# Another order of steps in the head and middle of a fused block: the last fold of Wk ahead of the first values

## The chip, the core and the metric

One core of a Trainium2 chip runs the whole program. Its engines work side by side, each through its own queue of instructions in order: TensorE (PE, with its weight loads as PEld), VectorE (DVE), ScalarE (ACT), GpSimd (POOL) and SyncE (SP), which issues nearly all DMA transfers. An instruction that waits holds everything behind it in its engine's queue. Matmul results go to PSUM, eight banks of 512 float32 numbers in each of 128 partitions; the other engines move them to SBUF. The metric is the device time of one execution in microseconds (us); lower is better. A measurement is a median over several executions.

## What is computed

A pre-norm transformer block with linear attention and a feed-forward part, on 2048 tokens of width 640 in bf16, with 32 heads of width 20:

```python
qkv = (layernorm(x) @ wqkv)                    # q, k, v: 32 heads of 20
pq, pk = q @ w_phi, k @ w_phi                  # a 20x20 matrix for each head
phi_q = concat(softmax(pq), softmax(-pq))      # 40 features
phi_k = concat(softmax(pk), softmax(-pk))
kv  = phi_k^T @ v                              # summed over all tokens
z   = sum over tokens of phi_k
o   = (phi_q @ kv) / (phi_q @ z + 1e-6)
h   = x + o @ wo
out = h + silu(layernorm(h) @ w1) @ w2         # inner width 1728
```

## The kernel before

**Tiles and stages.** Tokens come in 16 tiles of 128, the width in five chunks of 128. The stages overlap: a head (first 11 us or so) in which w_phi is multiplied into the key part of wqkv, so that keys come out as features at once; a middle (to about 68 us) that makes keys K and values V of each tile, exponentiates and scales the keys and adds them into kv (two PSUM banks, 6 and 7); then queries, attention, the out projection and the feed-forward part, which follow in the same list and run to the end.

**Order by hand.** Every piece of work is a named step, a small function that emits a few instructions. One string, ORDER (lines 18 to 61), lists all 897 names; line 1097 walks through it and calls each step. The scheduler is in manual mode, so each engine gets its instructions in exactly this order, and the semaphores that keep data right are put in by the framework. A name's place in the list therefore sets its place only in the queues of the engines that it uses. ON (line 159) says on which engine some steps run.

**Steps of the head.**
- `warm0` to `warm17` (line 231): matmuls of constants that only keep TensorE busy, two banks of kv as target.
- `X0`, `X1`, `X2`, `X4`, `X8` (line 178): loads of 1, 1, 2, 4 and 8 tiles of x. `WK0` to `WK4` and `WV0` to `WV4` (line 181): loads of the five chunks of Wk and Wv, 160 KB each. `wph0`, `wph1` (lines 379, 381), `wq0` to `wq5` (line 425): w_phi once more, and transposed loads of the query part. All are issued by SP; WPH, the first load of w_phi, by ACT (line 183).
- `phi_a`, `phi_b` (lines 305, 308): DVE spreads w_phi into blocks; phi_a begins with the difference WPD.
- `wkC` (line 321): five transposes of a chunk of Wk into PSUM; `wkeC` (line 338): its copy to WTk, on DVE or ACT; `fkC` (line 345): six matmuls of it with phi, the fold; `fkCe` (line 354): the copy to Wfk on ACT.
- `stT` (lines 478, 479): mean and variance of a tile on DVE, three instructions; `rsT`: the inverse deviation, on POOL with a power (lines 487, 490) or on ACT (484, 485); `xnT` (line 494): the normalised tile on DVE or POOL; `xtT`: its transpose, by TensorE for tiles 0 to 3 (line 530) with `xT` (line 550) as copy, by a DMA (line 552) for the others.
- `V0.C` (line 583): tile 0's values, chunk by chunk, two matmuls each that need chunk C of Wv; `K0.C` (line 598): the same for keys. `K0s` takes a pair of PSUM banks.

**Steps of the middle.** `KT`, `VT` (line 571): ten matmuls of a tile with Wfk or Wv; `exT` (line 626): two exponentials on ACT into one of five EK buffers; `suT` (line 630): their sums on DVE; `rkT` (lines 638, 639): inverses on ACT; `scT` (line 643): the scaling on DVE, in place; `veT` (line 647): values to SBUF on ACT; `kvT` (line 662): eleven matmuls of scaled keys and values; `refT` (line 247) and `onesT` (lines 250, 252, 247): constants in buffers, on POOL. `mask`, `mask0` and `own` are masks on POOL; `phq` (line 402 on) spreads w_phi for the queries on POOL; `fqR`, `fqRe` (lines 437, 443) fold it into the query weights; `load0` to `load10` (line 563) load wo, w1 and w2.

**PSUM.** Six of the eight banks go round in three pairs (line 124): each wk pair, fold, xt, K and V takes the next pair and waits until the copy or exponential that empties its former use is done. The order in which the steps stand in ORDER thus also decides which step waits for which copy.

Of the kernel before, what the change touches and what calls it, by code (L numbers as in the profile page):

```python
# [15 lines left out]


ORDER = """
warm0 warm1 warm2 warm3 warm4 warm5 warm6 warm7 warm8 warm9 warm10 warm11 warm12 warm13 warm14 warm15
warm16 X0 WK2 st0 wk2 ones5 WK3 phi_a warm17 WK0 wke2 X1 phi_b wk3 mask fk2 wke3 ones4 WK1 WK4 wk0 rs0  # L20
xn0 xt0 fk2e wk1 X2 WV0 WV3 st1 X4 wke0 wke1 WV2 fk3 wph0 wk4 ones0 rs1 ones3 fk3e WV1 pad0 ones1 x0
wke4 fk0 fk1 V0.0 fk0e fk4 xn1 xt1 V0.3 WV4 fk1e K0s K0.2 st2 st3 fk4e K0.1 wph1 x1 mask0 K0.0 st4 rs3
own K0.4 rs2 xn2 K0.3 ex0 K1 V0.2 rs4 xn3 st6 xt2 ex1 V0.1 wq3 V1 wq0 xt3 x2 rs6 V0.4 ve1 X8 st5 xn4 su0
xn6 su1 rk0 sc0 x3 xt4 st7 K2 ve0 V2 ex2 st9 rs5 wq1 xn5 st10 ve2 K3 xt5 kv0 ex3 rs7 V3 rk1 ve3 st8
ones2 sc1 phq xn7 su2 K4 ex4 st14 V4 fq0 V5 rs8 ve4 fq0e xt6 kv1 su3 rk2 ve5 rs9 fq3 ref6 fq3e sc2 wq2
ref5 K5 xt7 su4 K6 ex5 kv2 st11 V6 xn8 xn9 ex6 st12 rk3 ref7 fq2 sc3 wq4 su5 K7 ve6 rk4 xt8 xt9 fq2e ex7
sc4 V7 rs10 su6 xn10 kv3 rs11 rs12 fq1 V8 ve7 kv4 su7 fq1e zeros ref8 fq4 ve8 V9 rk5 K8 fq4e rk6 ref9
ve9 sc5 xn12 kv5 sc6 rk7 ex8 wq5 st13 K9 fq5 sc7 ones6 ex9 load7 xt10 kv6 rs14 ref10 xn11 rs13 fq5e su8
Q0 kv7 st15 su9 eqr0 rk8 K10 qe0 V10 xn13 sc8 Q1 xn14 rs15 ex10 qs0 xt12 V12 kv8 ve10 rk9 sc9 ref13 qe1
su10 load9 ql0 ve12 load3 qs1 rk10 sc10 xt11 ref12 kv9 ref11 xt13 K12 xn15 K11 ex12 su12 K13 load1 ex11  # L30
ex13 load10 V11 kv10 xt14 su11 K14 ql1 load4 qi0 ve11 eqr1 V13 rk11 eqp su13 qi1 rk12 sc11 kv11 qr1
ref14 xt15 rk13 qr0 sc12 K15 ex14 su14 load0 Q2 ve13 kv12 sc13 ref15 ex15 rk14 su15 qe2 V14 rk15 V15
ve14 load5 Q3 kv13 sc14 mask1 kv14 ve15 sc15 qt1 qs2 load2 kv15 bd0 Q7 qt0 ql2 load6 load8 qi2 Q5 qe3
halves bd1 D0 D1 qr2 qe7 qe5 Q4 qs3 ql3 E0 Q10 E1 qi3 qr3 qs5 qe4 qe10 qt2 Q6 ql5 D2 ot0 qs4 qe6 ot1 Q9
qi5 ql4 qi4 qr5 qt3 qt5 E2 G00 qe9 G01 ga0 lm0 qr4 G11 ot2 G10 ls0 Q11 lr0 D3 qs6 qe11 Q8 ga1 E3 lm1 qt4
hn0 qs7 ot3 D5 E5 ls1 Q13 G20 qe8 lr1 ht0 G21 hn1 qe13 Q14 ht1 ga2 Q15 qr6 qs8 qe14 Q12 G31 qe15 qr7 D4
G30 qr8 E4 ot5 qt6 qe12 u0.L padL0 T3.0 u0.4 ga3 u0.6 qs9 s0.L G50 G51 D6 T1.1 T1.2 ga5 lm2 s0.4 s0.6
ls2 qt7 lm5 T2.2 u0.0 u0.8 s0.0 T3.2 ot4 s0.8 D7 lr2 lm3 E6 u0.12 ls5 qt8 u0.2 s0.2 padL1 E7 T4.2 S3.0
G41 ls3 T1.0 ot6 T3.1 lr5 G40 u0.10 D8 ga4 p7.0 T2.1 E8 G61 hn2 ot7 T2.0 lt0 hn5 lr3 lm4 s0.12 T4.1 G60
T4.0 s0.10 p1.0 p2.0 G71 r7.0 S1.0 ht2 r1.0 S2.0 G70 qr9 ht5 p6.0 S4.0 ls4 hn3 p4.0 r2.0 lr4 p5.0 hn4  # L40
w11.0 p3.0 ga6 ht3 w21.0 ht4 u2.6 qs11 r3.0 u2.10 w22.0 qt9 u2.L u2.9 ot8 w12.0 s2.10 qr11 ga7 u2.7 qs10
lm6 s2.6 qr10 D9 ls6 qs12 G81 qt11 s2.7 s2.L u2.4 s2.9 u2.1 G80 E9 lm7 ga8 qr12 qt10 u2.5 s2.1 lm8 u2.3
lt2 qt12 qs13 u2.2 s2.5 s2.4 D10 s2.3 ls7 u2.0 s2.0 u2.12 E10 lr6 ot9 s2.12 ot10 D11 u2.8 qr13 s2.2
u2.11 qs14 E11 s2.8 s2.11 G90 S3.2 ls8 G91 D12 p7.2 qr14 G101 ga9 hn6 r7.2 S1.2 lm9 lr7 p1.2 qt13 ot11
D13 ls9 E12 S2.2 G100 lr9 lr8 hn7 p2.2 r1.2 qt14 p6.2 ga10 G110 w11.2 r2.2 p4.2 hn9 ht6 ot12 ht9 G111
ht7 E13 S3.4 D14 hn8 w21.2 S4.2 ga11 p5.2 w22.2 p7.4 lm11 ht8 r3.2 lm10 E14 ot13 ls10 S1.4 p1.4 r7.4
p3.2 r1.4 out0 S2.4 out1 G121 u6.L G120 p6.4 qs15 u6.8 ga12 G131 ot14 r2.4 p5.4 s6.8 qr15 lm12 ls11 G130
p4.4 w21.4 lr10 u6.12 ga13 out3 qt15 lr11 w22.4 out5 s6.12 u6.5 w12.2 G140 ls12 r3.4 D15 s6.L u6.4 lt6
hn10 lr12 ht10 hn11 G141 u6.0 ga14 E15 lm13 ls13 u6.11 s6.5 p2.4 s6.11 hn12 s6.4 u6.7 u6.10 u6.9 u6.2
s6.10 s6.2 u6.6 ot15 s6.0 s6.7 w11.4 lr13 G151 hn13 u6.3 s6.6 S4.4 ht11 ht12 s6.9 s6.3 G150 u6.1 ht13  # L50
p3.4 u10.L s6.1 S3.6 lm14 u10.7 ga15 u10.12 p7.6 s10.7 S3.8 S1.6 s10.L lt10 lm15 w12.4 ls14 u10.0 u10.2
p1.6 r1.6 u10.4 ls15 s10.2 out2 s10.12 u10.6 lr14 lr15 r7.6 hn15 hn14 S2.6 p6.6 S4.6 ht15 p2.6 s10.0
p4.6 r2.6 p3.6 p5.6 ht14 w21.6 u10.8 s10.4 r3.6 u10.3 u10.1 w22.6 w11.6 u14.L p7.8 s10.8 s10.3 w12.6
out4 s10.6 S1.8 r7.8 p1.8 u14.0 u10.10 u10.5 r1.8 s10.5 s14.L s10.1 out6 S2.8 p6.8 S4.8 u10.11 r2.8 p5.8
S3.10 u10.9 s10.9 p4.8 s10.11 w21.8 p2.8 u14.10 s14.0 w22.8 s10.10 r3.8 p3.8 p7.10 w11.8 u14.4 S1.10
u14.2 p2.10 p1.10 out7 S2.10 s14.2 w12.8 r7.10 s14.10 p4.10 u14.12 r1.10 p6.10 S4.10 u14.8 S3.12 s14.4
r2.10 w21.10 p5.10 S1.12 u14.6 p1.12 out9 w11.10 p3.10 S2.12 p2.12 r3.10 r1.12 s14.8 out8 w11.12 p6.12
# [1077 lines left out]
```

## Time and profile before

| | |
|---|---|
| median of 3 runs | 225.18 us (224.81 to 225.22) |
| the profiled execution's own time | 225.49 us |
| its span, first to last instruction | 223.8 us |
| granted TensorE clock, mean | 0.998 |
| TensorE busy | 218.2 us |
| DVE, ACT, POOL busy | 173.0, 144.4, 70.2 us |

The 1.7 us between the profiled time and its span lie before the first and behind the last instruction. Busy times are unions of an engine's instructions; ends of matmuls are modelled, so that a busy TensorE may still lose up to about 0.15 us between two matmuls unseen. In a timeline a row gives start and duration in us, engine, line, operation, what it writes and reads, the number of merged instructions, and in brackets the idle time before it and what ended that. In the rows of one line or tile three durations are minimum, median and maximum in ns.

### The profile page before, as it was taken

The numbers are of one execution on the slowest core, as the hardware profiler recorded it, in microseconds if no ns is written. First come the engines' busy times: TensorE is split into PE (matmuls) and PEld (weight loads), VectorE is DVE, ScalarE is ACT, GpSimd is POOL, SyncE is SP. The second block draws the span as 40 slices with busy tenths as digits, with TensorE's granted clock in tenths as the row PEclk, the third lists the DMA queues.
The fourth block names the chain that finished last, engine by engine and source line by source line (L and its number), as shares of the span: only waits on it lengthen the run. The fifth ranks groups of instructions, "written<-read, shape, count | busy, mean of one in ns | idle before, by whom it ended". The sixth has DMA issues, their size and how long they took to land.

```text
span 223.8 us, 5031 instructions
## 1 busy us (share of the span) xinstructions
PE 218.2 (98%) x1926; PEld 154.8 (69%) x1935; DVE 173.0 (77%) x305; ACT 144.4 (65%) x321; POOL 70.2 (31%) x136
## 2 busy tenths in 40 slices
PE   8799999999999999999999999999999999999994
PEld 5677777777777777887655577665455656778773
DVE  4899999999989999999999999944024344436694
ACT  2799999999979899997086774268568332321000
POOL 6789899899000130163020130132004000000000
PEclk9999999999999999999999999999999999999999
DMA  6994639679999874935536666434512410010012
GB/s 174 320 263 134 114 77 165 185 190 161 315 201 175 175 134 81 213 56 107 126 78 139 126 145 124 120 95 81 63 29 53 91 60 0 29 44 0 29 62 88
DMA packets 68158, 26.98 MB, mean 121 GB/s; under 512 B 61159, under 2 KB 67111, under 8 KB 68007
## 3 DMA queue, kind: packets, MB, share of 16 engines
q1 hardware_dynamic: 67335, 26.61, 53.3%
q8 instruction: 15, 0.25, 0.5%
q10 hardware_dynamic: 800, 0.06, 0.3%
q14 instruction: 8, 0.07, 0.1%
HBM read 9.55 MB, written 2.62 MB: 54 GB/s over the span
## 4 chain that ended last, share of the span: by engine, by line
PE 94%; DMA 2%; SPq 2%; issue 0%; DVE 0%
PE banks L931 25%; PE banks L1036 24%; PE banks L571 18%; PE banks L849 10%; PE banks L609 9%; PE banks L817 3%; PE banks L662 2%; DMA Wv<-in_A_wqkv_dram 2%; PE banks L942 1%; SPq L181 1%; PE banks L583 1%; PE banks L437 1%; PE banks L598 1%; SPq L178 1%; PE banks L530 0%
## 5 line engine op out<-in xcount | busy, mean ns | idle before, releaser
L931 PE MATMUL banks<-HnT,w_sb 128*128 128x512 bf16 (+1 forms) x316 | 60.0, 335 | 0.4
L954 ACT ACTIVATE shT<-banks 128x512 bf16<-128x512 f32 (+1 forms) x53 | 29.1, 586 | 45.8 <-PE banks L931 44.8
L931 PEld LDWEIGHTS <-w_sb 128*128 128x128 bf16 x325 | 31.2, 98 | 21.2
L571 PEld LDWEIGHTS <-XnT 128*128 128x128 bf16 x300 | 28.5, 98 | 9.5
L494 POOL TENSOR_SCALAR xn<-X,mv,rs 128x640 bf16<-128x640 bf16 x12 | 30.6, 2550 | 1.7 <-ACT rs L485 1.4
L1036 PEld LDWEIGHTS <-S 128*128 128x128 bf16 x224 | 21.6, 98 | 8.8
L1044 DVE TENSOR_TENSOR r<-banks,X 128x320 f32<-128x320 f32 x32 | 15.4, 487 | 15.7 <-PE banks L1036 13.2
L516 POOL TENSOR_SCALAR rs<-mv 128x1 f32<-128x1 f32 x16 | 3.9, 244 | 73.8 <-ACT xn L509 73.5
L1036 PE MATMUL banks<-T,S 128*128 128x320 bf16 x168 | 26.1, 299 | 0.0
L849 PE MATMUL banks<-wo_sb,OT 128*128 128x320 bf16 x160 | 25.5, 299 | 0.1
L737 DVE TENSOR_REDUCE Sq<-EQ 128x66 f32<-128x1320 bf16 x16 | 24.2, 1519 | 0.0
L609 PE MATMUL banks<-Wfq,XnT 128*128 128x342 bf16 (+2 forms) x160 | 22.7, 293 | 0.0
L571 PE MATMUL banks<-Wv,XnT 128*128 128x320 bf16 x150 | 22.7, 299 | 0.0
L1051 DVE TENSOR_TENSOR o_t<-banks,r 128x320 bf16<-128x320 f32 (+2 forms) x33 | 14.9, 473 | 9.9 <-PE banks L1036 9.6
L630 DVE TENSOR_REDUCE Sk<-EK 128x64 f32<-128x1216 bf16 x16 | 22.2, 1403 | 0.1
L733 ACT ACTIVATE EQ<-banks 128x342 bf16<-128x342 f32 (+2 forms) x52 | 21.5, 526 | 0.4 <-PE banks L609 0.3
L1036 PEld LDWEIGHTS <-shT 128*128 128x128 bf16 x175 | 16.8, 98 | 6.6
L571 PE MATMUL banks<-Wfk,XnT 128*128 128x304 bf16 x150 | 21.3, 292 | 0.0
L626 ACT ACTIVATE EK<-banks 128x608 bf16<-128x608 f32 x32 | 20.3, 697 | 1.0 <-PE banks L571 0.5
L849 PEld LDWEIGHTS <-OT 128*128 128x128 bf16 x160 | 15.3, 98 | 6.7
L1018 DVE TENSOR_TENSOR S<-shT 128x896 bf16<-128x896 bf16 x16 | 9.8, 619 | 12.5 <-ACT shT L954 8.8
L609 PEld LDWEIGHTS <-XnT 128*128 128x128 bf16 x160 | 15.0, 97 | 5.4
(97 smaller groups left out, 329.2 us busy)
## 6 DMA issues: line engine op xcount, KB each, us to landing
out_dram<-o_t SPq DMA_DIRECT2D x15, 160.0 KB, 1.8
w_sb<-in_B_w_dram SPq DMA_DIRECT2D x5, 432.0 KB, 5.7
w_sb<-in_B_w_dram SPq DMA_DIRECT2D x3, 480.0 KB, 6.6
X<-in_A_x_dram SPq DMA_DIRECT2D x1, 1280.0 KB, 5.9
Wk<-in_A_wqkv_dram SPq DMA_DIRECT2D x5, 160.0 KB, 3.5
Wv<-in_A_wqkv_dram SPq DMA_DIRECT2D x5, 160.0 KB, 5.8
wo_sb<-in_A_wo_dram SPq DMA_DIRECT2D x1, 800.0 KB, 5.1
X<-in_A_x_dram SPq DMA_DIRECT2D x1, 640.0 KB, 6.5
```

What stands on the lines that cost most here:

```text
L494: eng.tensor_scalar(out=xn_[t][:], in0=X[:, t, :], scalar1=mv_.pop(t)[:, 0:1], scalar2=rs_.pop(t)[:], op0=ALU.subtract, op1=ALU.mult,)
L571: nc.tensor.matmul(ps[:, g, 0:w], XnT[:, c, t * P : (t + 1) * P], W[:, c, g * w : (g + 1) * w], start=(c == 0), stop=(c == C - 1),)
L609: nc.tensor.matmul(ps[:, 0 : e - a], XnT[:, c, t * P : (t + 1) * P], Wfq[:, c, a:e], start=(c == 0), stop=(c == C - 1),)
L626: nc.scalar.activation(E5[:, :, :, b, 0:DR], p4, AF.Exp, scale=sign)
L630: nc.vector.tensor_reduce(sk[t][:], ek[t][:, 0 : H * HF].rearrange("p (q f) -> p q f", f=DH)[:, :, 0:DR], axis=AX.X, op=ALU.add)
L733: nc.scalar.activation(features(t, a, b)[:, :, :, i, 0:DR], p4, AF.Exp, scale=sign)
L737: nc.vector.tensor_reduce(sq[t][:], EQ[0][:, t, :, 0:FCH].rearrange("p c (q f) -> p c q f", f=DH), axis=AX.X, op=ALU.add)
L849: nc.tensor.matmul(ps_of["G", t][:, g, 0:HD], ot[t][:, c, :], wo_sb[:, c, g * HD : (g + 1) * HD], start=(c == 0), stop=(c == C - 1),)
L931: nc.tensor.matmul(ps[:, at : at + n], w1_sb[:, c, fc * P : fc * P + P], HnT[u][:, c, 0:n], start=(c == 0), stop=(c == C - 1),)
L954: nc.scalar.activation(rows_of(u)[:, f0 * n : f1 * n], ps_of.pop(("u", u, f0))[:, 0 : (f1 - f0) * n], AF.Silu)
L1036: nc.tensor.matmul(ps[:, lo:hi], left[:, c, :], right[:, c, lo:hi], start=(c == 0 and k in FIRST), stop=(c == KS - 1 and k in LAST), skip_ ...
L1044: nc.vector.tensor_tensor(r_[t, name][:], ps_of[bank, t][:, 0:HD], X[:, t + i, g * HD : (g + 1) * HD], op=ALU.add)
```

## The change

Only ORDER changes, and only its first third: the same 897 names, from the first up to `rk12 kv11 qr1 ref14 xt15` in other places, the rest (from `rk13` on) word for word as it was. No instruction is added or taken away. On TensorE the order changes from

```
... wk2 warm17 wk3 fk2 wk0 xt0 wk1 fk3 wk4 fk0 fk1 V0.0 fk4 xt1 V0.3 K0.2 K0.1 K0.0 K0.4 K0.3 K1
V0.2 xt2 V0.1 V1 xt3 V0.4 K2 V2 K3 kv0 V3 K4 V4 fq0 V5 kv1 fq3 K5 K6 kv2 ...
```

to

```
... warm17 wk2 wk3 fk2 wk0 xt0 wk1 fk3 wk4 fk0 fk1 fk4 xt1 V0.0 V0.3 K0.2 K0.1 K0.0 K0.4 K0.3 K1
V0.2 xt2 V1 V0.1 xt3 V0.4 V2 K2 K3 V3 kv0 kv1 V4 K4 fq0 V5 fq3 kv2 K5 K6 ...
```

On DVE phi_a comes ahead of st0, and xn2 ahead of st4. On SP the order of the first twelve loads (up to `X4 WV2`) stays; behind them it was `wph0 WV1 WV4 wph1 wq3 wq0 X8 xt4 wq1 xt5 ...` and becomes `WV1 WV4 wph1 wq0 X8 wph0 wq3 wq5 xt4 xt5 ...`; `load1`, `load10` and `load4` come earlier among the transposes xt10 to xt15, `load3` later. On POOL the memsets of `mask`, `ones0` and the mask's first side come ahead of rs0, those of `ones4`, `ones3` and `pad0` later.

```diff
-warm0 warm1 warm2 warm3 warm4 warm5 warm6 warm7 warm8 warm9 warm10 warm11 warm12 warm13 warm14 warm15
-warm16 X0 WK2 st0 wk2 ones5 WK3 phi_a warm17 WK0 wke2 X1 phi_b wk3 mask fk2 wke3 ones4 WK1 WK4 wk0 rs0
-xn0 xt0 fk2e wk1 X2 WV0 WV3 st1 X4 wke0 wke1 WV2 fk3 wph0 wk4 ones0 rs1 ones3 fk3e WV1 pad0 ones1 x0
-wke4 fk0 fk1 V0.0 fk0e fk4 xn1 xt1 V0.3 WV4 fk1e K0s K0.2 st2 st3 fk4e K0.1 wph1 x1 mask0 K0.0 st4 rs3
-own K0.4 rs2 xn2 K0.3 ex0 K1 V0.2 rs4 xn3 st6 xt2 ex1 V0.1 wq3 V1 wq0 xt3 x2 rs6 V0.4 ve1 X8 st5 xn4 su0
-xn6 su1 rk0 sc0 x3 xt4 st7 K2 ve0 V2 ex2 st9 rs5 wq1 xn5 st10 ve2 K3 xt5 kv0 ex3 rs7 V3 rk1 ve3 st8
-ones2 sc1 phq xn7 su2 K4 ex4 st14 V4 fq0 V5 rs8 ve4 fq0e xt6 kv1 su3 rk2 ve5 rs9 fq3 ref6 fq3e sc2 wq2
...
+warm0 warm1 mask warm2 warm3 warm4 warm5 warm6 phi_a warm7 warm8 warm9 warm10 warm11 warm12 ones5 warm13
+warm14 warm15 warm16 ones0 X0 WK2 WK3 warm17 wk2 st0 wk3 wke2 mask0 phi_b rs0 WK0 X1 WK1 wke3 xn0 fk2
+ones1 wk0 WK4 own xt0 st1 wk1 fk2e fk3 wke1 ones3 wke0 X2 WV0 x0 ones4 wk4 wke4 fk0 rs1 fk3e xn1 fk0e
+WV3 fk1 fk4 fk1e xt1 X4 K0s pad0 V0.0 fk4e st2 st3 rs2 V0.3 K0.2 WV2 x1 K0.1 K0.0 K0.4 rs3 K0.3 xn3 xn2
+ex0 WV1 st4 WV4 K1 rs4 xn4 V0.2 st5 wph1 ex1 wq0 xt2 V1 st6 V0.1 X8 x2 xt3 ve1 rs5 xn5 V0.4 x3 su0 V2
+rk0 K2 ve2 rs6 wph0 su1 wq3 st7 xn6 rk1 ve0 K3 ex2 wq5 ex3 xt4 V3 ve3 sc1 sc0 rs7 kv0 kv1 ones2 st8 xt5
+phq ref5 rs8 su2 xt6 wq2 wq1 xn7 rk2 st9 xt7 V4 sc2 ve4 su3 K4 fq0 xn8 V5 ex4 fq3 fq0e ref6 wq4 kv2 ve5
...
```

More of the change, by code (lines that the diff above doesn't have):

```diff
@@ L24 @@
-xn6 su1 rk0 sc0 x3 xt4 st7 K2 ve0 V2 ex2 st9 rs5 wq1 xn5 st10 ve2 K3 xt5 kv0 ex3 rs7 V3 rk1 ve3 st8
-ones2 sc1 phq xn7 su2 K4 ex4 st14 V4 fq0 V5 rs8 ve4 fq0e xt6 kv1 su3 rk2 ve5 rs9 fq3 ref6 fq3e sc2 wq2
-ref5 K5 xt7 su4 K6 ex5 kv2 st11 V6 xn8 xn9 ex6 st12 rk3 ref7 fq2 sc3 wq4 su5 K7 ve6 rk4 xt8 xt9 fq2e ex7
-sc4 V7 rs10 su6 xn10 kv3 rs11 rs12 fq1 V8 ve7 kv4 su7 fq1e zeros ref8 fq4 ve8 V9 rk5 K8 fq4e rk6 ref9
-ve9 sc5 xn12 kv5 sc6 rk7 ex8 wq5 st13 K9 fq5 sc7 ones6 ex9 load7 xt10 kv6 rs14 ref10 xn11 rs13 fq5e su8
@@ L29 @@
[L29 to L53, printed above, removed]
@@ L54 @@
-out4 s10.6 S1.8 r7.8 p1.8 u14.0 u10.10 u10.5 r1.8 s10.5 s14.L s10.1 out6 S2.8 p6.8 S4.8 u10.11 r2.8 p5.8
+warm0 warm1 mask warm2 warm3 warm4 warm5 warm6 phi_a warm7 warm8 warm9 warm10 warm11 warm12 ones5 warm13
+warm14 warm15 warm16 ones0 X0 WK2 WK3 warm17 wk2 st0 wk3 wke2 mask0 phi_b rs0 WK0 X1 WK1 wke3 xn0 fk2
+ones1 wk0 WK4 own xt0 st1 wk1 fk2e fk3 wke1 ones3 wke0 X2 WV0 x0 ones4 wk4 wke4 fk0 rs1 fk3e xn1 fk0e
+WV3 fk1 fk4 fk1e xt1 X4 K0s pad0 V0.0 fk4e st2 st3 rs2 V0.3 K0.2 WV2 x1 K0.1 K0.0 K0.4 rs3 K0.3 xn3 xn2
@@ new lines @@
+ex0 WV1 st4 WV4 K1 rs4 xn4 V0.2 st5 wph1 ex1 wq0 xt2 V1 st6 V0.1 X8 x2 xt3 ve1 rs5 xn5 V0.4 x3 su0 V2
+rk0 K2 ve2 rs6 wph0 su1 wq3 st7 xn6 rk1 ve0 K3 ex2 wq5 ex3 xt4 V3 ve3 sc1 sc0 rs7 kv0 kv1 ones2 st8 xt5
+phq ref5 rs8 su2 xt6 wq2 wq1 xn7 rk2 st9 xt7 V4 sc2 ve4 su3 K4 fq0 xn8 V5 ex4 fq3 fq0e ref6 wq4 kv2 ve5
+st12 su4 fq3e K5 rk3 rs9 K6 ex5 st11 sc3 V6 xt8 ex6 fq2 rk4 ve6 kv3 st10 K7 V7 xn9 ref7 su5 rs10 ref8
+fq2e xn10 xt9 fq1 ex7 ve7 fq1e load7 V8 zeros fq4 rs12 rk5 ve8 st13 load1 fq4e sc4 kv4 V9 su6 rk6 ve9
@@ new lines @@
+xn12 ref9 fq5 rs11 su7 K8 sc5 sc6 xt10 kv5 st14 K9 fq5e ones6 st15 eqr0 rs13 load9 ex8 kv6 Q0 xn11 rs14
+load10 su8 ex9 rk7 xt12 V10 qe0 ref10 rk8 xn13 xt11 K10 su9 rs15 sc7 V12 sc8 load4 rk9 ve10 qs0 Q1 ex10
+ve12 xt13 sc9 xn14 ref11 su10 kv7 xt14 ref12 qe1 ql0 qs1 K12 kv8 K11 ex12 kv9 K13 ref13 V11 rk10 ql1
+ex11 xn15 ex13 su12 sc10 qi0 kv10 ve11 load3 su11 ref14 K14 V13 rk11 su13 qi1 eqr1 sc11 kv11 eqp rk12
+xt15 qr1 rk13 qr0 sc12 K15 ex14 su14 load0 Q2 ve13 kv12 sc13 ref15 ex15 rk14 su15 qe2 V14 rk15 V15 ve14
@@ new lines @@
+load5 Q3 kv13 sc14 mask1 kv14 ve15 sc15 qt1 qs2 load2 kv15 bd0 Q7 qt0 ql2 load6 load8 qi2 Q5 qe3 halves
+bd1 D0 D1 qr2 qe7 qe5 Q4 qs3 ql3 E0 Q10 E1 qi3 qr3 qs5 qe4 qe10 qt2 Q6 ql5 D2 ot0 qs4 qe6 ot1 Q9 qi5 ql4
+qi4 qr5 qt3 qt5 E2 G00 qe9 G01 ga0 lm0 qr4 G11 ot2 G10 ls0 Q11 lr0 D3 qs6 qe11 Q8 ga1 E3 lm1 qt4 hn0 qs7
+ot3 D5 E5 ls1 Q13 G20 qe8 lr1 ht0 G21 hn1 qe13 Q14 ht1 ga2 Q15 qr6 qs8 qe14 Q12 G31 qe15 qr7 D4 G30 qr8
+E4 ot5 qt6 qe12 u0.L padL0 T3.0 u0.4 ga3 u0.6 qs9 s0.L G50 G51 D6 T1.1 T1.2 ga5 lm2 s0.4 s0.6 ls2 qt7
@@ new lines @@
+lm5 T2.2 u0.0 u0.8 s0.0 T3.2 ot4 s0.8 D7 lr2 lm3 E6 u0.12 ls5 qt8 u0.2 s0.2 padL1 E7 T4.2 S3.0 G41 ls3
+T1.0 ot6 T3.1 lr5 G40 u0.10 D8 ga4 p7.0 T2.1 E8 G61 hn2 ot7 T2.0 lt0 hn5 lr3 lm4 s0.12 T4.1 G60 T4.0
+s0.10 p1.0 p2.0 G71 r7.0 S1.0 ht2 r1.0 S2.0 G70 qr9 ht5 p6.0 S4.0 ls4 hn3 p4.0 r2.0 lr4 p5.0 hn4 w11.0
+p3.0 ga6 ht3 w21.0 ht4 u2.6 qs11 r3.0 u2.10 w22.0 qt9 u2.L u2.9 ot8 w12.0 s2.10 qr11 ga7 u2.7 qs10 lm6
+s2.6 qr10 D9 ls6 qs12 G81 qt11 s2.7 s2.L u2.4 s2.9 u2.1 G80 E9 lm7 ga8 qr12 qt10 u2.5 s2.1 lm8 u2.3 lt2
@@ new lines @@
+qt12 qs13 u2.2 s2.5 s2.4 D10 s2.3 ls7 u2.0 s2.0 u2.12 E10 lr6 ot9 s2.12 ot10 D11 u2.8 qr13 s2.2 u2.11
+qs14 E11 s2.8 s2.11 G90 S3.2 ls8 G91 D12 p7.2 qr14 G101 ga9 hn6 r7.2 S1.2 lm9 lr7 p1.2 qt13 ot11 D13 ls9
+E12 S2.2 G100 lr9 lr8 hn7 p2.2 r1.2 qt14 p6.2 ga10 G110 w11.2 r2.2 p4.2 hn9 ht6 ot12 ht9 G111 ht7 E13
+S3.4 D14 hn8 w21.2 S4.2 ga11 p5.2 w22.2 p7.4 lm11 ht8 r3.2 lm10 E14 ot13 ls10 S1.4 p1.4 r7.4 p3.2 r1.4
+out0 S2.4 out1 G121 u6.L G120 p6.4 qs15 u6.8 ga12 G131 ot14 r2.4 p5.4 s6.8 qr15 lm12 ls11 G130 p4.4
@@ new lines @@
+w21.4 lr10 u6.12 ga13 out3 qt15 lr11 w22.4 out5 s6.12 u6.5 w12.2 G140 ls12 r3.4 D15 s6.L u6.4 lt6 hn10
+lr12 ht10 hn11 G141 u6.0 ga14 E15 lm13 ls13 u6.11 s6.5 p2.4 s6.11 hn12 s6.4 u6.7 u6.10 u6.9 u6.2 s6.10
+s6.2 u6.6 ot15 s6.0 s6.7 w11.4 lr13 G151 hn13 u6.3 s6.6 S4.4 ht11 ht12 s6.9 s6.3 G150 u6.1 ht13 p3.4
+u10.L s6.1 S3.6 lm14 u10.7 ga15 u10.12 p7.6 s10.7 S3.8 S1.6 s10.L lt10 lm15 w12.4 ls14 u10.0 u10.2 p1.6
+r1.6 u10.4 ls15 s10.2 out2 s10.12 u10.6 lr14 lr15 r7.6 hn15 hn14 S2.6 p6.6 S4.6 ht15 p2.6 s10.0 p4.6
@@ L55 @@
+r2.6 p3.6 p5.6 ht14 w21.6 u10.8 s10.4 r3.6 u10.3 u10.1 w22.6 w11.6 u14.L p7.8 s10.8 s10.3 w12.6 out4
+s10.6 S1.8 r7.8 p1.8 u14.0 u10.10 u10.5 r1.8 s10.5 s14.L s10.1 out6 S2.8 p6.8 S4.8 u10.11 r2.8 p5.8
 S3.10 u10.9 s10.9 p4.8 s10.11 w21.8 p2.8 u14.10 s14.0 w22.8 s10.10 r3.8 p3.8 p7.10 w11.8 u14.4 S1.10
```

## The prediction, before the result

> **What bounds the kernel now.** I read the page first, then busy time by stretch, then the view of waits, and last the timeline of the first 11 us.
>
> ```profile
> span 223.8 us, 5031 instructions
> ...
> PE 218.2 (98%) x1926; PEld 154.8 (69%) x1935; DVE 173.0 (77%) x305; ACT 144.4 (65%) x321; POOL 70.2 (31%) x136
> ```
>
> ```profile
> 0.00:5.00 5.00, 4.17 (x23) 2.91 (x23) 1.69 (x5) 1.28 (x1) 3.05 (x19) 1.00 0.59 153
> 5.00:10.00 5.00, 3.60 (x50) 3.14 (x51) 4.40 (x13) 3.99 (x8) 4.31 (x18) 1.00 0.96 324
> ...
> 20.00:30.00 10.00, 10.00 (x108) 7.59 (x106) 9.83 (x21) 9.51 (x24) 8.92 (x13) 1.00 0.52 100
> ```
>
> The columns after each stretch's length are PE, PEld, DVE, ACT and POOL. TensorE is the bound: from 20 to 30 us it is busy throughout, and 0 to 10 us holds idle time of it. There DVE and ACT are at 95% or more as well, so little spare is left if a step comes late. The list of waits has one entry of TensorE that is worth winning; the second row below is taken up later.
>
> ```profile
> PE banks L583 <- DMA Wv<-in_A_wqkv_dram: 1.1, 1, 1.1
> ...
> PEld L662 <- DVE EK L643: 0.3, 1, 0.3
> ```
>
> ```profile
> 4.72 0.27 PE L231 MATMUL banks<-const-bfloat16-1.0 128*128 128x256 bf16 x1
> 5.25 0.45 PE L321 MATMUL banks<-ident,Wk 128*128 128x128 bf16 x5 [0.25 <-DMA Wk<-in_A_wqkv_dram]
> 5.61 0.70 PE L345 MATMUL banks<-phi,WTk 128*128 128x228 bf16 x6
> ...
> 6.47 0.45 PE L530 MATMUL banks<-ident,xn 128*128 128x128 bf16 x5
> ...
> 7.72 1.07 PE L345 MATMUL banks<-phi,WTk 128*128 128x228 bf16 x12
> 9.94 0.43 PE L583 MATMUL banks<-Wv,XnT 128*128 128x320 bf16 x2 [1.15 <-DMA Wv<-in_A_wqkv_dram]
> 10.21 0.54 PE L345 MATMUL banks<-phi,WTk 128*128 128x228 bf16 x6
> ...
> 10.87 0.43 PE L583 MATMUL banks<-Wv,XnT 128*128 128x320 bf16 x2
> ```
>
> Step V0.0 (line 583) stands at 9.94 us until the first chunk of Wv lands. Behind it come fk4 (10.21) and xt1, which need nothing of that load, then V0.3 (10.87).
>
> **The head: fk4 and xt1 ahead of V0.0.** They take 10.87 - 10.21 = 0.66 us, which is all that can move into the wait: the loads up to Wv's second chunk keep their order on SP, so V0.0 cannot go before 9.90 (4.54 + 5.36 below), and V0.3's chunk, issued 0.47 later with at least 5.3 to landing, is there at about 10.36.
>
> ```profile
> 4.54 5.36 DMA Wv<-in_A_wqkv_dram
> ...
> DMA to landing us min/median/max: 5.3/5.8/6.5
> ```
>
> But they gain only if TensorE reaches them in time, and another edit of the change delays it. On DVE, st0 (the moments of tile 0) goes behind the two instructions of phi_a, and wke2 stays behind both:
>
> ```profile
> DMA to landing us min/median/max: 2.7/2.7/2.7
> ...
> 0.78 0.48 ACTq L183 DMA_DIRECT2D WPH<-in_A_w_phi_dram  x1
> 3.16 0.89 DVE L478 BATCH_NORM_STATS2 st<-X 128x6 f32<-128x320 bf16 x2 [3.16 <-DMA X<-in_A_x_dram]
> 4.08 0.21 DVE L479 BATCH_NORM_AGGREGATE mv<-st 128x2 f32<-128x12 f32 x1
> 4.21 0.20 DVE L305 TENSOR_TENSOR WPD<-WPH 128x95 bf16<-128x95 bf16 x1
> 4.39 0.23 POOL L487 TENSOR_SCALAR rs<-mv 128x1 f32<-128x1 f32 x1 [1.05 <-DVE mv L479]
> 4.52 0.63 DVE L308 TENSOR_TENSOR phi<-WPD,own 128x456 bf16<-128x456 bf16 x1
> 4.70 0.89 POOL L490 TENSOR_TENSOR rs<-rs,nhalf_t 128x1 f32<-128x1 f32 x1
> 5.08 0.48 DVE L338 COPY WTk<-banks 128x640 bf16<-128x640 bf16 x1
> 5.86 0.56 DVE L494 TENSOR_SCALAR xn<-X,mv,rs 128x640 bf16<-128x640 bf16 x1
> ```
>
> WPH lands at 0.78 + 2.7 = 3.5; WPD 0.2, phi_a 0.63 and st0 1.13 (3.16 to 4.29) follow, so the moments are there at 5.4 instead of 4.29. rs0 on POOL took 5.59 - 4.29 = 1.30, of which 0.89 was the power. Its fastest of five was 0.56 (row below), so it ends at 6.4 to 6.7, and xn0 (0.56) at 7.0 to 7.3.
>
> ```profile
> L490 POOL TENSOR_TENSOR rs<-rs,nhalf_t x5: 561/568/887, 4.7 to 49.0; 128x1 f32<-128x1 f32 x5
> ```
>
> xt0 on TensorE follows 0.05 later as before (6.42 to 6.47): at 7.0 to 7.3 instead of 6.47. What stands ahead of it does not fill that: wke2 ends at 5.4 + 0.48 = 5.9, and fk2 and wk0 together last 6.47 - 5.61 = 0.86, until 6.75. From xt0 through wk1, fk3, wk4, fk0 and fk1 the old run lasted from 6.47 to about 8.67 (the x12 group's last matmul starts at 8.57 by 7.72 + 1.07 less its 0.22), 2.2 us. With the 0.66 of fk4 and xt1, V0.0 can start at 9.9 to 10.15; I add 0.15 as an estimate for a PSUM pair, as five steps in a row now take one of three pairs while ACT needs 0.6 to empty a fold that TensorE makes in 0.38. So V0.0 starts at 9.95 to 10.3 and V0.3 0.27 later, not before 10.36: 10.4 to 10.6 where it was 10.87. The head gains 0.25 to 0.5; I take 0.35.
>
> The row of the power, 0.89 beside phi_a against 0.56 elsewhere, is where the Trainium skill bears on this. Its GPSIMD Engine Reference (Specifications) says GpSimd's way to SBUF is shared with VectorE and is contended by DVE instructions with two SBUF inputs; here that is phi_a before, and phi_b, also two tensors, after. By that rule the power stays at 0.89 and the head gains the lower 0.25; without it, 0.5. The 0.35 above rests on neither.
>
> **The middle: kv0.** K2, K3, V3 now precede kv0 (V3 stood behind it), and kv0 is the first step that waits for a scaled EK. From V0.3 TensorE has K0 and K1 (1.29 each), V0.2, V0.1, V0.4 (0.27 each), xt2 and xt3 (0.28), V1, V2, V3 (1.36) and K2, K3 (1.30), and V0.3 itself 0.27: 10.9 us, which from 10.4 to 10.6 gives 21.3 to 21.5 (the same sum without V3 gives 10.87 + 9.54 = 20.41, where kv0 stood).
>
> ```profile
> 12.03 0.89 DVE L478 BATCH_NORM_STATS2 st<-X 128x6 f32<-128x320 bf16 x2 [0.40 <-DMA X<-in_A_x_dram]
> 13.55 0.87 DVE L478 BATCH_NORM_STATS2 st<-X 128x6 f32<-128x320 bf16 x2
> 14.59 0.83 DVE L478 BATCH_NORM_STATS2 st<-X 128x6 f32<-128x320 bf16 x2
> 15.58 1.36 DVE L630 TENSOR_REDUCE Sk<-EK 128x64 f32<-128x1216 bf16 x1
> 16.86 0.92 DVE L494 TENSOR_SCALAR xn<-X,mv,rs 128x640 bf16<-128x640 bf16 x1
> 17.71 1.40 DVE L630 TENSOR_REDUCE Sk<-EK 128x64 f32<-128x1216 bf16 x1
> 19.03 1.14 DVE L643 TENSOR_TENSOR EK<-EK,Rk 128x1280 bf16<-128x1280 bf16 x1
> 20.40 0.50 PE L662 MATMUL banks<-VP,EK 128*128 128x63 bf16 x11
> ...
> L643 DVE TENSOR_TENSOR EK<-EK,Rk x16: 769/816/1136, 19.0 to 62.9; 128x1280 bf16<-128x1280 bf16 x16
> ```
>
> On DVE the new order is st4, st5, st6, su0, su1, st7, xn6, sc1, sc0, then kv0 may go. From X4's landing (12.03, its place in the queue unchanged) three moments at 1.04 give 15.15, two sums at 1.33 (17.71 to 19.03) 17.8, st7 18.85, xn6 0.5 to 0.9 (its 0.92 stood beside a normalise of POOL) 19.35 to 19.75, two scales at 0.75 to 1.1: 20.9 to 21.9. TensorE is ready at 21.3 to 21.5, so kv0 waits 0 to 0.6. I take 0.15, nearest to xn6 at 0.9 and scales at the median 0.82. Behind kv0 on TensorE wait kv1, V4, K4 and all that follow. Against it stands the 0.3 that the weight load of one kv step (line 662) waits for its scale in the list of waits. It is kv2. In the new order DVE does st8, su2, st9 (3.4) and sc2 (0.8) after sc0's 21.3, until 25.5, while TensorE goes through kv0, kv1 (0.34 each), V4, K4, fq0, V5 and fq3 (0.25 each fq) from 21.5 until 26.7. So this wait goes: 0 to 0.3, as part of it lay under matmuls still running; I take 0.13. For the later steps up to xt15, which keep nearly all intervals of one engine but change places by a step or two, the trace shows no TensorE wait at all; I allow 0.1, with 0 and 0.4 as bounds (0.4 is one late ACT copy or exponential of 0.7 that half hides).
>
> **What costs nothing, and its cover.** warm17 now runs before wk2, 0.1 to 0.2, but wk3 must wait for its load at 5.25 anyway. POOL's memsets of mask, ones and pad0 change places inside its 1.05 idle before rs0 and behind it; without that cover they would cost rs0 their 0.2 to 0.7. On SP, X8 goes ahead of the larger load of w_phi and one transposed load of Wq, so it is issued no later than before:
>
> ```profile
> 12.73 0.65 SPq L178 DMA_DIRECT2D X<-in_A_x_dram  x1
> ...
> X<-in_A_x_dram SPq DMA_DIRECT2D x1, 1280.0 KB, 5.9
> ...
> 21.38 0.65 POOL L402 TENSOR_TENSOR WPQD<-WPQ 120x95 bf16<-120x95 bf16 x2
> ```
>
> That load then lands right behind X8, by 12.73 + 5.9 = 18.6 or little more, and POOL first reads it at 21.4: some 2.5 us of cover, without which phi_q and fq0 wait. The loads of w1 and w2 go a few steps earlier or later on SP among the transposes xt10 to xt15; one that came late behind a load would hold the K or V of its tile. The old order has such loads among them too and no wait of TensorE for a transpose; this lies in the 0 to 0.4 of the rest.
>
> **Sum.** -0.35 (head) + 0.15 (kv0) - 0.13 (kv2) + 0.1 (rest) = -0.23 us of the profiled execution's 225.49, thus 225.26. The median of three is 225.18, 0.31 lower, so I forecast 225.18 - 0.2 = 225.0 us. A measurement of this kernel tells 0.2%, 0.45 us, from no change, so this counts as no change.
>
> **Rivals.** (a) The head keeps the whole move and the middle waits for nothing: rs0's power at 0.56, V0.3 at 10.4, kv2's 0.13 gone: -0.5 to -0.65, 224.6 us. For it: kv0 and the scales have spare if xn6 takes its shorter 0.5; against it: the power's 0.89, and that the gain's ceiling is 0.66. (b) Slower: DVE's chain to kv0 decides. If xn6 and both scales run beside POOL's normalises as 16.86 and 19.03 did, and rs0 keeps its 0.89, sc0 ends at 21.9 to 22.1 while TensorE is ready at 21.4: 0.6, and as DVE and ACT have no room until 30 us, a second such loss of 0.3 follows; less 0.25 from the head, +0.6, 225.8 us. It decides once sc0 ends later than 21.75. For it: 98% busy DVE; against it: of 16 scales the median is 0.82, and DVE starts st4 without xn2's 0.47 in its way. (c) The load of Wv lands at another time than in the profiled execution: 0.5 earlier, and the old order would have lost less while the new stands at its own chain, +0.3; later, and the full 0.66 is won. It is hidden in (a) and (b).
>
> **How the numbers follow.** No change near -0.2: 0.50. Rival (a) 0.26, rival (b) 0.24; (c) spreads over both. The likeliest case alone spans 224.75 to 225.55; to hold 8 in 10 the range reaches down to 224.6 and up to 225.8. Faster by over 0.2% 0.26, within 0.50, slower 0.24.
>
> **What would show it.** Right: fk4 and xt1 ahead of V0.0, xt0 at 7.0 to 7.3, V0.0 near 10.1 with a wait for Wv under 0.2, V0.3 at 10.4 to 10.6; kv0 at 21.3 to 21.7; the waits for Wv gone from the list and a short one for DVE xn in the head in their place. Wrong: xt0 at 6.5 (st0 did not delay it), kv0 with a wait over 0.5, or any TensorE wait over 0.4 between 22 and 70 us.

## The result, and the profile after

| | before | changed |
|---|---|---|
| median of 20 runs | 225.16 us (224.47 to 225.61) | 225.45 us (225.44 to 226.23) |
| the profiled execution's own time | 225.49 us | 225.46 us |
| its span | 223.8 us | 223.7 us |

By the medians the changed kernel is slower by 0.29 us. The ratio of the runs is given as 1.0018, with a 95% interval of 1.001 to 1.0026; it is not the quotient of the two medians, which is 1.0013, but both say slower. Two things in this table matter more than the medians. The profiled executions differ by only -0.03 us. And the changed kernel repeats itself: 17 of its 20 runs lie between 225.44 and 225.48, while those of the kernel before are spread over 1.14 us.

First the page of the changed kernel and its busy time by stretch; the columns are as before (length, PE, PEld, DVE, ACT, POOL, clock, DMA share, GB/s).

```profile
span 223.7 us, 5052 instructions
...
PE 218.6 (98%) x1935; PEld 154.7 (69%) x1935; DVE 173.1 (77%) x305; ACT 144.6 (65%) x321; POOL 70.4 (31%) x136
```

```profile
0.00:5.00 5.00, 3.99 (x23) 2.88 (x23) 1.41 (x3) 1.28 (x1) 3.12 (x18) 1.00 0.58 147
5.00:10.00 5.00, 3.88 (x54) 3.26 (x55) 4.47 (x13) 3.31 (x7) 3.76 (x18) 1.00 1.00 329
20.00:30.00 10.00, 10.00 (x110) 7.79 (x108) 9.90 (x18) 9.72 (x24) 9.60 (x13) 1.00 0.57 89
```

The middle is full as it was. The head still has idle time on TensorE, 1.12 us from 5 to 10 us where it was 1.40. Its waits have other names now; after each name stand the total, the count and the longest:

```profile
PE banks L345 <- DVE WTk L338: 0.5, 1, 0.5
PE banks L321 <- DMA Wk<-in_A_wqkv_dram: 0.5, 1, 0.5
PE banks L530 <- DVE xn L494: 0.4, 1, 0.4
```

The wait for Wv (line 583) is gone, and so is kv2's wait for its scale (line 662). In their place TensorE waits for DVE: for wke2's copy and for xn0. The timeline of the changed kernel shows how that came about:

```profile
3.22 0.70 POOL L262 TENSOR_SCALAR_AFFINE_SELECT mask<-mask 128x378 f32<-128x378 f32 x1
3.48 0.52 DVE L305 TENSOR_TENSOR WPD<-WPH 128x95 bf16<-128x95 bf16 x1 [3.48 <-DMA WPH<-in_A_w_phi_dram]
4.66 0.88 DVE L478 BATCH_NORM_STATS2 st<-X 128x6 f32<-128x320 bf16 x2
5.58 0.21 DVE L479 BATCH_NORM_AGGREGATE mv<-st 128x2 f32<-128x12 f32 x1
6.06 0.47 DVE L308 TENSOR_TENSOR phi<-WPD,own 128x304 bf16<-128x304 bf16 x1
6.19 0.76 POOL L490 TENSOR_TENSOR rs<-rs,nhalf_t 128x1 f32<-128x1 f32 x1
6.98 0.50 DVE L494 TENSOR_SCALAR xn<-X,mv,rs 128x640 bf16<-128x640 bf16 x1 [0.46 <-POOL rs L490]
7.54 0.45 PE L530 MATMUL banks<-ident,xn 128*128 128x128 bf16 x5 [0.37 <-DVE xn L494]
8.77 1.52 PE L345 MATMUL banks<-phi,WTk 128*128 128x228 bf16 x18
9.56 0.63 POOL L258 MEMSET w_sb<- 64x640 bf16 x1
9.58 0.79 DVE L494 TENSOR_SCALAR xn<-X,mv,rs 128x640 bf16<-128x640 bf16 x1
10.42 0.45 PE L530 MATMUL banks<-ident,xn 128*128 128x128 bf16 x5
10.71 0.71 PE L583 MATMUL banks<-Wv,XnT 128*128 128x320 bf16 x4
```

The x4 of the last row is V0.0 and V0.3 together, so V0.3 starts 0.27 later, at 10.98. The first chunk of Wv had landed at 9.36: V0.0 at 10.71 waits for no load any more, but for its own chain, st0 to rs0 to xn0 to xt0 and on to xn1 and xt1. Two rows of that chain are longer than in the kernel before: WPD took 0.52 (0.20 before), xn1 0.79 (0.43 before). Each lies beside a POOL instruction that had just begun: the select of `mask0` (3.22) and the memset of `pad0` (9.56).

The middle of the changed kernel, from the timeline:

```profile
19.04 2.51 POOL L494 TENSOR_SCALAR xn<-X,mv,rs 128x640 bf16<-128x640 bf16 x1
19.50 0.59 DVE L494 TENSOR_SCALAR xn<-X,mv,rs 128x640 bf16<-128x640 bf16 x1
20.01 1.55 DVE L643 TENSOR_TENSOR EK<-EK,Rk 128x1280 bf16<-128x1280 bf16 x2
20.51 1.52 PE L571 MATMUL banks<-Wv,XnT 128*128 128x320 bf16 x10
21.87 0.84 PE L662 MATMUL banks<-VP,EK 128*128 128x63 bf16 x22
27.06 0.50 PE L662 MATMUL banks<-VP,EK 128*128 128x63 bf16 x11
```

Both scales are done at 20.01 + 1.55 = 21.56, 0.31 before TensorE has finished V3. kv0, kv1 (21.87) and kv2 (27.06) start without a wait.

### The profile page after: what moved, and what is told of

Its sections match the earlier page's. It is cut to its first block, busy times and chain, and to the rows that moved or that the text cites. A ratio compares the mean times of both kernels' runs of the same rounds, so it can differ in the third digit from the quotient of the medians.

```text
span 223.7 us, 5052 instructions
## 1 busy us (share of the span) xinstructions
PE 218.6 (98%) x1935; PEld 154.7 (69%) x1935; DVE 173.1 (77%) x305; ACT 144.6 (65%) x321; POOL 70.4 (31%) x136
## 4 chain that ended last, share of the span: by engine, by line
PE 94%; DVE 3%; DMA 1%; POOL 0%; issue 0%; DVEq 0%
PE banks L931 25%; PE banks L1036 24%; PE banks L571 18%; PE banks L849 10%; PE banks L609 9%; PE banks L817 3%; PE banks L662 2%; DMA WPH<-in_A_w_phi_dram 1%; PE banks L942 1%; DVE st L478 1%; PE banks L437 1%; PE banks L583 1%; PE banks L598 1%; DVE xn L494 1%; PE banks L530 0%; DVE WTk L338 0%
## 5 line engine op out<-in xcount | busy, mean ns | idle before, releaser
L931 PE MATMUL banks<-HnT,w_sb 128*128 128x512 bf16 (+1 forms) x325 | 61.0, 336 | 0.0
```

Source lines behind the costliest of these rows:

```text
L931: nc.tensor.matmul(ps[:, at : at + n], w1_sb[:, c, fc * P : fc * P + P], HnT[u][:, c, 0:n], start=(c == 0), stop=(c == C - 1),)
```

## The experiments

All kernels differ from one of the two only in ORDER. In the diffs "..." stands for names left as they are. The first question was which of the two moves in the head costs the time, st0 behind phi_a or V0.0 behind fk4 and xt1, and whether the middle costs anything. Each is undone or done alone; the kernel before had 225.12 us in these runs.

**st0 first again.** Changed kernel with:

```diff
-... warm6 phi_a warm7 ... wk2 st0 wk3 ...
+... warm6 warm7 ... wk2 st0 phi_a wk3 ...
```

> The changed kernel with one step moved: phi_a behind st0, as it stood before the change. Theory A (the head chain: st0 behind phi_a holds back rs0, xn0 and xt0 by 1.07 us, from 6.47 to 7.54, so that fk4, xt1 and V0.0 come when the load of Wv has long landed): xt0 at 6.5 again, V0.0 within 0.2 of its load's landing or at 9.6, V0.3 at 10.0 to 10.4, and the time 0.2 to 0.6 under the kernel before, 224.6 to 225.0. Theory B (the new order of the middle costs the 0.3): xt0 at 6.5 too, but waits of TensorE behind 12 us that make it 225.3 or more.

Measured: 224.86 us (224.41 to 225.91), ratio to the kernel before 0.9982 (0.9969 to 0.9996). Its timeline:

```profile
4.12 0.21 DVE L305 TENSOR_TENSOR WPD<-WPH 128x95 bf16<-128x95 bf16 x1
...
6.75 0.44 PE L530 MATMUL banks<-ident,xn 128*128 128x128 bf16 x5
...
8.73 0.47 DVE L494 TENSOR_SCALAR xn<-X,mv,rs 128x640 bf16<-128x640 bf16 x1
...
10.40 0.43 PE L583 MATMUL banks<-Wv,XnT 128*128 128x320 bf16 x2 [0.16 <-DMA Wv<-in_A_wqkv_dram]
```

xt0 came at 6.75, not at the 6.5 expected, but V0.3 comes 0.58 earlier and the time falls by 0.59. WPD and xn1 are short again; both fall at other times against POOL. V0.3 waits for its load once more: the head is at the load's pace, and the runs are spread again.

**st0 late in the old order.** Kernel before with:

```diff
-warm16 X0 WK2 st0 wk2 ones5 WK3 phi_a warm17 ...
+warm16 X0 WK2 wk2 ones5 WK3 phi_a st0 warm17 ...
```

> The kernel before with st0 moved behind phi_a, nothing else. Theory A: xt0 at 7.5, V0.0 not before 9.7 however early its load lands, so the time is 225.2 to 225.5 and its fast runs (under 224.9) are gone, as in the changed kernel. Theory B: the head has 1.3 us of idle time ahead of V0.0 that covers this, so the time is that of the kernel before, 225.16, with the same spread.

Measured: 225.64 us, 1.0019 (1.0009 to 1.0029), all 12 runs between 225.54 and 225.69. That is a little above the range of theory A. The move of st0 alone costs about 0.5 us by the medians (225.12 in the kernel before) and makes the time constant. Here WPD stands beside nothing of POOL (0.26), but xn0 is caught:

```profile
6.63 0.80 DVE L494 TENSOR_SCALAR xn<-X,mv,rs 128x640 bf16<-128x640 bf16 x1 [0.46 <-POOL rs L490]
...
6.96 0.29 POOL L247 MEMSET EK<- 128x64 f32 x1
```

**V0.0 back ahead of fk4.** Changed kernel with:

```diff
-WV3 fk1 fk4 fk1e xt1 X4 K0s pad0 V0.0 fk4e ...
+WV3 fk1 V0.0 fk4 fk1e xt1 X4 K0s pad0 fk4e ...
```

> The changed kernel with V0.0 put back ahead of fk4 and xt1. Theory A: the load has landed when TensorE comes to V0.0 in either order, so the move is worth nothing here: V0.0 at 10.0 to 10.2, V0.3 at 10.9 to 11.0, time 225.45 within 0.15. If fk4 and xt1 ahead of V0.0 did gain what was forecast for them (0.25 to 0.5), this is slower by that: 225.7 or more.

Measured: 225.23 us (225.21 to 226.45), 1.0008 (0.9994 to 1.0022). This was a miss: I expected no gain from undoing the move, and it gained 0.22. With st0 late nothing waits for Wv at 9.9, so the move has nothing to win; what it loses is V0.0 as cover. In the changed kernel the folds end at 8.77 + 1.52 = 10.29 and xt1 stands until xn1 is done; with V0.0 between them that time is used. V0.3 stands here at 10.86, 0.12 earlier:

```profile
10.86 0.43 PE L583 MATMUL banks<-Wv,XnT 128*128 128x320 bf16 x2
```

Where the other 0.10 comes from is not shown, as the profile caught a longer execution.

That execution, 226.45, was one of two of the 12 that came in over 226 us. It shows where its time went:

```profile
16.93 2.83 SPq L425 DMA_TRANSPOSE WTq<-in_A_wqkv_dram  x1
...
19.88 4.23 SPq L552 DMA_TRANSPOSE XnT<-xn  x3
...
23.53 1.53 PE L571 MATMUL banks<-Wv,XnT 128*128 128x320 bf16 x10 [0.95 <-DMA XnT<-xn]
```

X8 landed at 20.14 (18.38 in the changed kernel's profile), the transposed loads of Wq behind it held SP until 19.76, xt4 was issued after them, and V4 waited 0.95 us. The changed kernel had one run of that length in 20 (226.23); it was not profiled.

**Both head moves undone**, the rest of the change left (st0 as in the first experiment, V0.0 as here).

> The changed kernel with st0 ahead of phi_a and V0.0 ahead of fk4: the head of the kernel before with the middle of the changed one. Theory A (the middle costs nothing and saves kv2's wait of 0.13): 224.95 to 225.2, with a spread of runs as before the change. Theory B (the middle costs): 225.3 to 225.5.

Measured: 224.81 us (224.32 to 225.97), 0.9982 (0.9967 to 0.9997). This is under the range of theory A. With the head's two moves taken out, the rest of the change is worth 0.3 us instead of costing anything. With st0 early no difference is seen between the two places of V0.0 (224.86 against 224.81). In both profiles V0.3 started 0.04 behind the landing of its own chunk of Wv (10.36 and 10.44), which V0.0's place does not change.

The next four (kernel before: 225.23) ask what makes the late st0 so dear, and how much of the result is the kernel before itself.

**POOL's two instructions elsewhere.** Changed kernel, st0 still late, with:

```diff
-... wk3 wke2 mask0 phi_b ... xn0 fk2 ones1 wk0 ... K0s pad0 V0.0 ...
+... wk3 wke2 phi_b ... xn0 fk2 ones1 pad0 mask0 wk0 ... K0s V0.0 ...
```

> The changed kernel with two instructions of POOL elsewhere: the first side of the mask and the pad of w2 (memset of w_sb, line 258) now come behind rs0, off the time of WPD (line 305) and xn1 (line 494) on DVE. In the changed kernel WPD took 0.52 with the mask's select beside it (0.20 before) and xn1 0.79 with the pad's memset beside it (0.44 before). Theory A1 (POOL beside them holds DVE up): WPD 0.2 to 0.3, xn1 0.45 to 0.55, xt0 at 7.2 to 7.3, V0.0 at 10.2 to 10.4, time 225.45 - 0.3 to 0.5, so 224.95 to 225.15. Rival (these two are slow for another reason): WPD, xn1 and the time stay, 225.45.

Measured: 225.07 us (225.04 to 225.41), 0.9995 (0.9984 to 1.0006). From its timeline:

```profile
3.45 0.26 DVE L305 TENSOR_TENSOR WPD<-WPH 128x95 bf16<-128x95 bf16 x1 [3.45 <-DMA WPH<-in_A_w_phi_dram]
...
7.28 0.45 PE L530 MATMUL banks<-ident,xn 128*128 128x128 bf16 x5 [0.36 <-DVE xn L494]
...
9.32 0.44 DVE L494 TENSOR_SCALAR xn<-X,mv,rs 128x640 bf16<-128x640 bf16 x1
9.50 0.86 POOL L395 MEMSET phi_q<- 128x684 bf16 x1
...
10.33 0.71 PE L583 MATMUL banks<-Wv,XnT 128*128 128x320 bf16 x4
```

Only POOL's instructions moved, and two DVE instructions became 0.26 and 0.35 shorter, V0.3 0.38 earlier (10.60) and the time 0.38 lower than the changed kernel's 225.45. Against the kernel before this kernel shows no difference.

**Wv earlier.** The first experiment, with both first loads of Wv ahead of X2 on SP:

```diff
-... wke0 X2 WV0 x0 ... fk0e WV3 fk1 ...
+... wke0 WV0 WV3 X2 x0 ... fk0e fk1 ...
```

> The changed kernel with phi_a behind st0 (as in the first run) and the loads WV0 and WV3 issued ahead of X2. Theory C (with st0 first the time follows the landing of Wv and X, which differs from one execution to the next): WV0 lands 0.6 to 1.0 earlier, V0.3 no longer waits (0.3 in the first run), V0.3 at 10.0 to 10.2, time 0.1 to 0.4 under the first run's 224.86, and its upper runs (225.0 to 225.1) gone. Rival (the landing of these two is not what spreads the runs): time and spread as in the first run.

Measured: 225.62 us (224.65 to 227.56), 1.0023 (1.0001 to 1.0046), a miss. Wv's chunks landed at 7.78 and 8.55, but X2 at 10.53 instead of 8.3 to 9.5. The moments that need X2 hold ACT up until 12.71 (11.52 in the first experiment), the exponentials behind them come later, and the loss shows on TensorE as a wait for one of them:

```profile
14.46 1.52 PE L571 MATMUL banks<-Wv,XnT 128*128 128x320 bf16 x10 [0.40 <-ACT EK L626]
```

In this execution, what one load gained was paid by another; over the runs the spread grew.

**The move alone.** Kernel before with:

```diff
-wke4 fk0 fk1 V0.0 fk0e fk4 xn1 xt1 V0.3 ...
+wke4 fk0 fk1 fk0e fk4 xn1 xt1 V0.0 V0.3 ...
```

> The kernel before with V0.0 moved behind fk4 and xt1, nothing else: the one edit that was to bring the gain, alone. By the prediction's head sum without the delay of st0: V0.3 at 10.3 to 10.4, 0.5 earlier, and 224.6 if nothing takes it back. Theory D: xn2 stands behind st4 on DVE, which waits for X4, so xt2 is not ready when TensorE comes 0.5 earlier, and the gain is given back there as a wait of about 0.5 ahead of xt2 (line 530 near 13.7): 225.1, no change.

Measured: 224.98 us (224.76 to 225.49), 0.9987 (0.997 to 1.0005): unclear, as 0.25 us is inside the interval. V0.3 stood at 10.21, but the first chunk of Wv had landed at 8.91 in this execution, 1.0 earlier than in the first profile, so how much of that is the move's cannot be read here. Some time goes at xt2, which comes before xn2 is done:

```profile
13.65 0.45 PE L530 MATMUL banks<-ident,xn 128*128 128x128 bf16 x5 [0.15 <-DVE xn L494]
```

**The kernel before once more**, unchanged, for a second profile.

> The kernel before, unchanged, for a second profile. Theory C: the wait ahead of V0.0 ends with the landing of WV0, and an execution's time is 225.49 plus the difference of that landing to 9.90, within 0.15. Rival: time and landing do not go together.

Measured: 225.19 us.

```profile
PE banks L583 <- DMA Wv<-in_A_wqkv_dram: 0.5, 1, 0.5
```

```profile
9.50 0.43 PE L583 MATMUL banks<-Wv,XnT 128*128 128x320 bf16 x2 [0.49 <-DMA Wv<-in_A_wqkv_dram]
...
10.43 0.43 PE L583 MATMUL banks<-Wv,XnT 128*128 128x320 bf16 x2
```

The same load, issued at 4.55 (4.54 in the first profile), landed at 9.45 instead of 9.90; the wait was 0.5 instead of 1.1, V0.3 0.44 earlier, and the time 0.30 lower (the other 0.14 went again behind V0.3). By theory C the time would have been 225.04, so 225.19 lies at the edge of its 0.15. The first profile had caught a late load: 9.90 is the latest landing in the eleven profiles with this order of loads.

Two last kernels tried to put the parts together (kernel before: 225.09).

**st0 first, POOL's two instructions as above, and X8 behind `wph0` and `wq3` on SP.**

```diff
-... V0.1 X8 x2 ... wph0 su1 wq3 st7 ...
+... V0.1 x2 ... wph0 su1 wq3 X8 st7 ...
```

> The changed kernel with the three delays of the runs so far taken out together: phi_a behind st0, the mask's first side and the pad of w2 behind rs0 on POOL, and X8 behind wph0 and wq3 on SP, where it stood before. Theory A (the head chain alone made the change slower, the rest of it gains): xt0 at 6.4 to 6.5, V0.3 set by its load at 9.9 to 10.4, time as the first run or a little under it, 224.6 to 224.9, spread by the landing of Wv, without runs over 225.5. Rival (the chain of ACT's folds or the X4 load holds the head at the same place anyway): 224.9 to 225.1.

Measured: 224.94 us (224.82 to 225.22), 0.9995 (0.9986 to 1.0003). None of 11 runs was over 225.22. That does not show X8's place to be the cause of the rare long runs: the kernel with POOL's two instructions elsewhere, with X8 in its new place, had none over 225.41 in 12, and the kernel before, with X8 in its old place, had two of 29 at 226.34 and 226.74 beside it. The time is not below the first experiment, and the timeline shows a reason: POOL's memsets, shifted, now meet xn1.

```profile
8.91 0.92 DVE L494 TENSOR_SCALAR xn<-X,mv,rs 128x640 bf16<-128x640 bf16 x1
```

```profile
9.36 0.30 POOL L247 MEMSET EK<- 128x64 f32 x1
```

**The move alone, with xn2 ahead of st4**, so that xt2 finds it ready. Kernel before with:

```diff
-... fk1 V0.0 fk0e fk4 xn1 xt1 V0.3 ... K0.0 st4 rs3 own K0.4 rs2 xn2 K0.3 ...
+... fk1 fk0e fk4 xn1 xt1 V0.0 V0.3 ... K0.0 own rs2 xn2 st4 rs3 K0.4 K0.3 ...
```

> The kernel before with V0.0 behind fk4 and xt1, and xn2 ahead of st4 on DVE (own and rs2 ahead with it, POOL's order unchanged): the run of the move alone showed a wait of 0.32 at xt2. Theory D (xn2 behind X4's load took the gain back): that wait goes, time 0.2 to 0.5 under the kernel before, 224.6 to 224.95. Rival: kv2 or another step of the old middle takes it back, 225.0 to 225.2.

Measured: 224.85 us (224.58 to 226.56), 0.9997 (0.9981 to 1.0013). From its timeline:

```profile
9.88 0.86 PE L583 MATMUL banks<-Wv,XnT 128*128 128x320 bf16 x4
...
29.37 0.40 PEld L662 LDWEIGHTS <-EK 128*128 128x128 bf16 x11 [0.46 <-DVE EK L643]
```

The first chunk of Wv landed at 9.84 here, about as late as in the first profile, and V0.3 started at 10.30 instead of 10.87: with st0 early and the load late the move gains 0.57 in the head, near the 0.66 that the prediction named as its ceiling. xt2's wait is gone, but kv2's wait for its scale is there, and the execution took 225.19. Whether the move alone helps the old order as a whole stays open. The two versions with the lowest ratio are the first experiment and the one with both head moves undone, each at 0.9982, about 0.3 us under the kernel before and 0.6 us under the changed one.

## Why the prediction was wrong

225.0 us was forecast, 225.45 measured. The steps against the profiles, in us from the span's start:

| point | before | forecast | changed | POOL apart | st0 first |
|---|---|---|---|---|---|
| tile 0's moments ready | 4.29 | 5.4 | 5.79 | 5.49 | 4.21 |
| rs0's power ends | 5.59 | 6.4 to 6.7 | 6.95 | 6.70 | 5.50 |
| xt0 starts | 6.47 | 7.0 to 7.3 | 7.54 | 7.28 | 6.75 |
| V0.0 starts | 9.94 | 9.95 to 10.3 | 10.71 | 10.33 | 9.81 |
| V0.3 starts | 10.87 | 10.4 to 10.6 | 10.98 | 10.60 | 10.40 |

Two steps of the prediction failed, both in the term of the head, forecast at -0.35.

**The first is the cover of POOL's moved instructions**, in "what costs nothing": it was checked against rs0 on POOL alone, not against what DVE does at that time. (The memset of `mask` stood ahead of rs0 in both orders; what came ahead of it is the select of `mask0`.) The fifth column shows the price: with that select and the memset of `pad0` out of the way, the forecast's points hold, the first and fourth within 0.1, and the time is 225.07. The collisions cost 0.26 up to xt0 and another 0.12 up to V0.0, 0.38 in all. The delay by st0 itself was seen rightly, and it is the smaller part: V0.3 at 10.60 with POOL apart against 10.40 with st0 first is 0.20 of the 0.58 between the changed kernel and the first experiment.

**The second is the point that the gain was counted from, as rival (c) had it.** V0.3 at 10.87 and 225.49 us belong to one execution with a late load of Wv, 0.33 above the median of its kernel. In the second profile, whose 225.19 lies near that median, the load landed at 9.45 and V0.3 stood at 10.43. From there the forecast's own 10.4 to 10.6 is no gain at all. Subtracting 0.2 from the median took the wait for the late load to be in every execution. The new order stands at its own chain, 1.35 us behind the load (9.36 and 10.71), and cannot gain when the load is early. Rival (c) was named with +0.3, but was not given a chance of its own; once the forecast had V0.0 at the new kernel's own pace, it should have had one.

So the head term came out at 10.98 - 10.87 = +0.11 against the first profile, and at 10.98 - 10.43 = +0.55 against the second. Of the 0.90 between -0.35 and +0.55, the late load is 0.44, the collisions are 0.38, and 0.08 is V0.3 at 10.60 instead of 10.52 without them. Neither failure alone makes the kernel slower: against the late execution, the changed kernel with its collisions differs by -0.03, and without the collisions (POOL apart) its time is not above the kernel before.

**The middle was priced too high.** It was given +0.15 (kv0), -0.13 (kv2) and +0.1 (the rest), +0.12 in all. The kv0 sum was right: V0.3 and 10.9 us give 10.98 + 10.9 = 21.88, and kv0 stands at 21.87. But the scales were done at 21.56, so there was no wait, and none either where V0.3 stood at 10.40 (kv0 at 21.28, scales done at 20.83). kv2's wait went as forecast, and the list shows no TensorE wait in the later steps. The time of an execution less the start of V0.3 gives the rest of the kernel alone. It is 214.48 in the changed kernel and 214.45 to 214.47 in four of the runs with its middle; in the kernel before it is 214.62 and 214.76, and in the three other runs with the old middle 214.72 to 214.89. (V0.0 back and Wv earlier are left out, as their waits of 0.95 and 0.40 fell behind V0.3.) These are single executions, but the two groups do not overlap: the new middle gains 0.14 or more, and 0.28 against the second profile, as both head moves undone showed at the medians (0.3). Which of the moved steps bring that, beyond kv2's wait, is not shown.

Against the second profile the sum is thus +0.55 in the head and -0.28 behind it, +0.27, where the medians have +0.29. That the time came within 0.45 of the forecast is partly luck: the middle, priced too high by 0.40, hid that much of the head's miss. The prediction also held that a measurement could not tell 0.45 us from no change; with 20 runs it told 0.29.

Rival (b), DVE's chain to kv0, did not happen: sc0 ended at 21.56, before the 21.75 that it needed. Rival (a) had the middle right and the head wrong.

The rule of the Trainium skill that the prediction weighed was aimed at one instruction only, the power. It took 0.76, between the 0.56 and the 0.89 considered. What cost time here were two DVE instructions: WPD, which has two inputs in SBUF, and xn1, which has one and so lies outside the rule as the prediction told it. The next section but one has the rows.
